# Reordering the start of a fused attention and MoE kernel by priorities, sharing one ring of buffers, and pairing its weighted sums

## The chip, the cores and the metric

The kernel runs on one core of one Trainium2 chip. The metric is the device time of one execution in microseconds (us); the kernel before took 1592.88 us, the median of three runs (1592.11 to 1593.0). The engines are TensorE (PE; its weight loads are shown as PEld), VectorE (DVE), ScalarE (ACT), GpSimd (POOL) and SyncE (SP). SP issues every transfer of this kernel, in one queue.

## The reference

Two layers of attention with 32 inducing points, and then a feed-forward block, over x of 4 batches of 12480 tokens of 128 channels:

```python
def mab(q, kv):
    s = scale * (q @ kv.transpose(0, 2, 1))
    s = s - s.max(-1, keepdims=True)
    a = np.exp(s)
    a /= a.sum(-1, keepdims=True) + 1e-09
    return a @ kv
h = mab(I, x)          # I: 32 x 128, the same for each batch; h: 32 x 128 a batch
y = mab(x, h)          # 12480 x 128 a batch
hid = y @ w_in         # 128 -> 2048
g = hid * (1.0 / (1.0 + np.exp(-1.702 * hid)))
out = g @ w_out        # 2048 -> 128
```

Everything is float32 on the device; w_in and w_out arrive as 64-bit floats and are decoded from their bits there. The first softmax runs over all tokens of a batch, so nothing of a batch's second softmax can start before h of that batch is known.

## The kernel before, in words

**Units.** A batch is cut into seven sups: six of 2048 tokens (four groups of 512, on four quarters of the partitions) and one of 192 (two groups of 96). A block is 512 tokens on their way through the feed-forward part. A batch gives 24 blocks, and the small sups of two batches make one more of 384 tokens, 98 blocks in all. y is never formed: y @ w_in is a @ (h @ w_in), so each batch needs `hw` = h @ w_in and the weights a of the second softmax, both as 32-bit values split into two fp32r parts and stacked on 128 partitions (`st` for a block, `hw` for a quarter of w_in).

**A block.** It has eight groups; a group `first(i)` (line 1022) makes two 128 x 512 hidden products into `ph`, ACT applies the gelu to get `g`, ACT or DVE rounds it to `hi`, and DVE takes the rest `lo`. `second(i, c)` (line 1052) adds three products to the block's output bank: hi with the low part of w_out, lo with the high part, hi with the high part. The first block (`WHOLE` = 8 groups) uses `g` and w_out undivided, as float32 products. `under_way` holds the half groups whose second products are still to be listed; `LAG` - 2 = 12 is the most, and the ring `ph_` has `LAG // 2` buffers each for hi and lo.

**Attention of a batch.** `attention(b)` (line 486) loads x transposed into the ring `px` (four buffers of one sup), makes the first scores `pa` with products of 32 output rows (four side by side, each on its own quarter of PE's columns), takes the maximum over all tokens (`max_turned`, `max_row`, `max_back`, `max_scaled`, lines 372 to 394), exponentials (`first_exponential`), transposes within 32 x 32 squares (`aT_of`), and a weighted sum `weigh` (line 409) against x by rows, which is loaded into the ring `pn` (two buffers), one sup after the other. `normalised` gives hT. `all_h_w_in` (line 592) makes `hw` of batches 1 to 3 and copies it into its stacked place by 16 transfers. `second_softmax` (line 562) makes second products in pairs of sups, and its exponentials four and three at a time.

**The start.** `start` (line 688) does the same for batch 0 with everything shown to it at once: x transposed stays in four buffers of `px` and two of its own, x by rows is made on the chip by PE's transposes for sups 0, 1, 2, 3 and 5 (`turning`, line 809; ACT copies them out), and loaded for sup 4 and the small one. The softmax is taken in two parts, sups 0 to 3 (`ES` = 4) with a first maximum and the others with the maximum over all; `joining` (line 867) rescales. The weights are decoded (`decode`, line 747) as their halves arrive, on ACT and DVE.

**What sets the order.** All instructions of an engine run in the order in which the program lists them. `Meter` and `Clocks` keep a planned time for each engine, from costs written in the kernel (`tensor_cost`, line 190). In the start, each piece of work is a generator that yields the engine and the tiles it needs next (`Jobs.add`). `Jobs.step` (line 145) lists the piece with the smallest planned time plus rank times 300 ns, over all engines. While PE would be idle by plan, `spin` (line 969) fills in dummy products `spun`, each charged 214 ns. After the start the main loop lists first and second groups and advances one generator, `attentions` (line 1090), a step a group; `until`, `room`, `deep` and `hop` hold it back. `deep` waits for a full queue of half groups before exponentials. `lay_out` (line 1119) runs the rest of it without pauses (`late`) if the weights of a sup are not there 14 groups ahead of their use.

Of the kernel before, what the change touches and what calls it, by code (L numbers as in the profile page):

```python
# [17 lines left out]
P = 128  # L18
# [4 lines left out]
LAG = 14  # L23
# [5 lines left out]
ES = 4  # L29
XB = 4  # L30
FB = 5
RANK = 300.0
# [98 lines left out]
class Jobs:  # L131
# [13 lines left out]
    def step(self, limit=None, but=None):  # L145
        best = None
        for job in self.threads:
            eng, tiles, when = job[1]
            if eng is but or when is not None and not when():
                continue  # L150
            t = max(eng.t, self.clocks.ready(*(tiles() if callable(tiles) else tiles)))
            if limit is not None and t > limit(eng):
                continue
            if best is None or t + job[2] * RANK < best[0]:
                best = t + job[2] * RANK, t, job
        if best is None:
            return False
        if self.idle:
            self.idle(best[1])
        job = best[2]  # L160
# [11 lines left out]
def set_attention_then_moe(ctx: ExitStack, tc, xT, x, indT, w_in, w_out, outT):  # L172
# [17 lines left out]
    def tensor_cost(name, out, w, x, **k):  # L190
        n = width(out)
        before, tiled[0] = tiled[0], out.shape[0] <= 32
        turn = 90 if before != tiled[0] else 0
        if x.dtype == F32R:
            return turn + max(107, 0.4548 * n)
        if name == "transpose":
            return turn + 0.85 * n
# [27 lines left out]
    NS = len(sups)  # L225
    EB = NS + 2
    on_chip = [s for s in range(NS - 1) if s != XB]

# [7 lines left out]
    pn = ctx.enter_context(tc.tile_pool(name="pn", bufs=2))  # L236
# [17 lines left out]
    rep2 = rep.rearrange("p g m -> p (g m)")  # L254
    one = const.tile([1, 1], F32, name="one")
# [17 lines left out]
    def deep():  # L273

        while len(under_way) < LAG - 2 and not late[0]:
            yield
# [32 lines left out]
    def load_xT(b, s):  # L309
        t0, g, w = sups[s]  # L310
        if g == G:
# [24 lines left out]
    def new_batch(b):  # L336
        a = SimpleNamespace(b=b, s1={}, aTs={})
# [29 lines left out]
    def first_max(a, s, scores):  # L367
        t0, g, w = sups[s]
        q = 32 * g
        dve.tensor_reduce(a.mx[0:q, s:s + 1], scores[0:q, 0:w], axis=AX.X, op=ALU.max)  # L370

    def max_turned(mx1):
        pa = ps_a.tile([P, 512], F32, tag="pa", name="pa")
        pe_.matmul(pa[0:1, 0:P], mx1, ident, start=True, stop=True)
        return pa

    def max_row(pa):
        row = psm.tile([1, M], F32, tag="row", name="row", bufs=1)
        dve.tensor_reduce(
            row, pa[0:1, 0:P].rearrange("p (g m) -> p m g", g=G), axis=AX.X, op=ALU.max  # L380
        )
        return row

    def max_back(row):
        pa = ps_a.tile([P, 512], F32, tag="pa", name="pa")
        for j in range(G):
            pe_.matmul(pa[32 * j:32 * j + 32, 0:1], row, one, start=True, stop=True)
        return pa

    def max_scaled(pa):  # L390
        nmx = psm.tile([P, 1], F32, tag="nmx", name="nmx")
        dve.tensor_scalar(nmx, pa[:, 0:1], -scale, None, op0=ALU.mult)
        return nmx

    def first_exponential(a, s, nmx):
# [3 lines left out]
        act.activation(e, e, AF.Exp, bias=nmx[0:q], scale=scale, accum_out=a.rs[0:q, s:s + 1])  # L399
# [86 lines left out]
    def attention(b):  # L486
# [26 lines left out]
        pa = max_turned(mx1)  # L513
        yield
        row = max_row(pa)
        yield from hop()
        pa = max_back(row)
# [8 lines left out]
        yield from until(dve, clocks.ready(a.s1[0][0]))  # L526
        yield from hop()
        pa = ps_a.tile([P, 512], F32, tag="pa", name="pa")
        aT_of(a, 0)
        xn = load_x(b, 0)  # L530
        yield from hop()
        i = 0
        for s in range(NS):
            if s == 2:
# [4 lines left out]
            if s + 1 < NS:  # L539
                yield from until(dve, clocks.ready(a.s1[s + 1][0]))  # L540
                yield from room()
                aT_of(a, s + 1)
                later = load_x(b, s + 1)
            yield from until(pe_, clocks.ready(a.aTs[s], xn))
            i = weigh(a, pa[:, 0:P], s, xn, i, blocks(range(NS)))
            xn = later
            yield from hop(3)
            if s < XB:
                again(b, s)
            yield from hop(3)  # L550
# [11 lines left out]
    def second_softmax(b, some):  # L562

        mine = {}
        for pair in pairs(some):
# [6 lines left out]
            pas = [second_products(b, s) for s in pair]  # L572
            yield
            for s, pa in zip(pair, pas):
                if s + XB < NS:
# [16 lines left out]
    def all_h_w_in(b):  # L592
# [6 lines left out]
        yield  # L599
# [9 lines left out]
        for c in range(G):  # L609
            t = phw.tile([P, 512], F32R, tag="hw", name="hw")  # L610
            for r in range(G):
                src = th.bitcast(F32) if r < G // 2 else tl
                sp.dma_start(
                    t[32 * r:32 * r + 32].bitcast(F32), src[32 * c:32 * c + 32]
                )
            hw[b, c] = t
            yield

# [69 lines left out]
    def start(pf, pw):  # L688
        a = new_batch(0)
        raws = []  # L690

        def load_out():

            t = pn.tile([P, BLK, P], F32, tag="xn", name="raw")
            for i in range(2):
                c = len(raws) - DFF // WC
                raws.append(t.rearrange("p k c -> p (k c)").bitcast(I32)[:, 2 * WC * i:2 * WC * (i + 1)])
                sp.dma_start(raws[-1], w_out[:, c * WC:(c + 1) * WC].bitcast(I32))

        for s in range(NS - 1):  # L700
            if s < DFF // WC:
                raws.append(pw.tile([P, 2 * WC], I32, tag="raw", name="raw", bufs=3))
                sp.dma_start(raws[s], w_in[:, s * WC:(s + 1) * WC].bitcast(I32))
            if s < XB:
                load_xT(0, s)
# [3 lines left out]
            if s == XB - 1:  # L709
                load_xT(0, NS - 1)  # L710
        turned = {}
        x5 = pn.tile([P, BLK, P], F32, tag="xn", name="xn")
        load_out()
        for s in range(XB, NS):
# [503 lines left out]
```

## Time and profile before

| | us |
|---|---|
| median of three runs | 1592.88 |
| span of the profiled execution, first to last instruction | 1591.5 |
| PE busy in it (matmuls are pipelined, so this is not PE at its peak) | 1580.0 |
| ACT busy | 1362.8 |
| DVE busy | 1318.4 |
| second products of batch 0 start at | 42.70 |
| first hidden product at | 50.51 |
| first divided product (hi with the low part of w_out) at | 72.66 |

The page gives no separate time for the profiled execution beside its span; the span lies 1.4 us below the median of the runs. In the rows below, "issue" names time in which an engine waited for nothing that the profile shows. Rows of groups have the count, the busy time, the mean of one in ns, and the idle time ahead with what ended it. All instructions listed through the `Meter` carry line 113, so tiles, not lines, tell them apart.

### The profile page before, as it was taken

To read this page: it belongs to the slowest core of one execution; us is meant where nothing else is said; L and a number is where in the kernel's file an instruction comes from. 1 tells how busy PE (TensorE), PEld (TensorE's weight loads), DVE (VectorE), ACT (ScalarE), POOL (GpSimd) and SP (SyncE) were. 2 spreads that over 40 slices of the span, in tenths; PEclk is the share of its full clock that TensorE was granted. 3 is DMA by queue.
4 is the path that set the end of the run, shared out by engine and by line. 5 is a ranking of instruction groups with operands and counts; after the bars stand their busy time and mean duration, and the time that the engine had idled before them with its cause. 6 is when DMAs were issued, how large, how long until landed. Compare 5 with 4: busy or idle time off the path is not lost.

```text
span 1591.5 us, 21955 instructions
## 1 busy us (share of the span) xinstructions
PE 1580.0 (99%) x7842; PEld 1236.7 (78%) x7842; DVE 1318.4 (83%) x1515; ACT 1362.8 (86%) x1573; POOL 0.7 (0%) x6
## 2 busy tenths in 40 slices
PE   9999999999999999999999999999999999999999
PEld 7667777777687778777777777777778788888887
DVE  6887987888888887788887887888878888888886
ACT  6789989987888888988888988988888998888885
POOL 0000000000000000000000000000000000000000
PEclk9999999999999999999999999999999999999999
DMA  7121415822242014731314112671311011111100
GB/s 270 60 65 69 155 34 114 189 58 55 83 162 78 21 47 109 172 87 35 105 44 175 49 34 51 149 165 37 93 44 48 24 42 41 35 32 40 39 29 20
DMA packets 85242, 125.71 MB, mean 79 GB/s; under 512 B 12176, under 2 KB 52880, under 8 KB 79504
## 3 DMA queue, kind: packets, MB, share of 16 engines
q1 hardware_dynamic: 85136, 124.32, 27.9%
q8 instruction: 64, 1.05, 0.3%
q14 instruction: 42, 0.34, 0.1%
HBM read 71.06 MB, written 25.56 MB: 61 GB/s over the span
## 4 chain that ended last, share of the span: by engine, by line
PE 96%; ACT 2%; DVE 1%; DMA 0%; issue 0%; SPq 0%; POOLq 0%; ACTq 0%; POOL 0%
PE pso L113 67%; PE ph L113 23%; PE pa L113 5%; PE spun L972 1%; ACT L113 1%; DVE lo L113 1%; DMA raw<-in_w_out 0%; ACT g L113 0%; PE h L113 0%; ACT hi L113 0%; ACT e L113 0%; DVE hi L113 0%; DVE e L113 0%; SPq L128 0%; DVE m L113 0%
## 5 line engine op out<-in xcount | busy, mean ns | idle before, releaser
L113 DVE TENSOR_TENSOR lo<-g,hi 128x1024 fp32r<-128x1024 f32 x776 | 939.0, 1217 | 162.8 <-ACT hi L113 148.1
L113 ACT ACTIVATE g<-ph 128x1024 f32<-128x1024 f32 (+1 forms) x784 | 810.4, 1038 | 180.0 <-PE ph L113 103.2
L113 PE MATMUL pso<-hi,wl 128*128 128x512 f32 (+1 forms) x1552 | 614.2, 396 | 0.0
L113 PE MATMUL pso<-lo,wh 128*128 128x512 f32 (+1 forms) x1552 | 608.1, 392 | 2.0 <-DVE lo L113 1.9
L113 PE MATMUL pso<-hi,wh 128*128 128x512 f32 (+1 forms) x1552 | 609.8, 393 | 0.0
L113 ACT ACTIVATE hi<-ph 128x1024 fp32r<-128x1024 f32 (+1 forms) x492 | 508.1, 1033 | 0.0
L113 PE MATMUL ph<-st,hw 128*128 128x512 f32 x1536 | 481.8, 398 | 2.7 <-ACT g L113 2.4
L113 PEld LDWEIGHTS pso<-hi,wl 128*128 128x128 f32 x1552 | 291.6, 188 | 82.3 <-issue 12.1
L113 PEld LDWEIGHTS ph<-st,hw 128*128 128x128 f32 x1536 | 286.5, 188 | 83.2 <-ACT g L113 12.4
L113 PEld LDWEIGHTS pso<-lo,wh 128*128 128x128 f32 x1552 | 291.8, 188 | 67.0 <-DVE lo L113 3.7
L113 PEld LDWEIGHTS pso<-hi,wh 128*128 128x128 f32 x1552 | 291.5, 188 | 66.7
L113 DVE CAST hi<-g 128x1024 fp32r<-128x1024 f32 x284 | 195.1, 687 | 75.9 <-ACT g L113 74.3
L113 ACT COPY ob<-pso 128x512 f32<-128x512 f32 (+1 forms) x98 | 59.2, 605 | 15.7 <-PE pso L113 15.7
L113 ACT ACT_TABLE_LOAD x30 | 38.5, 1283 | 1.2 <-PEq L1208 0.7
L972 PEld LDWEIGHTS spun<-ident 128*128 128x128 f32 x152 | 21.0, 214 | 7.0 <-issue 5.6
L113 PE MATMUL pa<-xt,hT 128*32 128x512 f32 x192 | 24.2, 600 | 1.7 <-DVE e L113 1.6
L972 PE MATMUL spun<-ident 128*128 128x128 f32 x152 | 23.5, 305 | 1.4 <-POOL ident masks.py:199 1.4
L113 PE MATMUL pa<-xt,indT_sb 128*32 128x512 f32 x192 | 23.7, 600 | 0.0
L113 PEld LDWEIGHTS pa<-xn,aT 128*32 128x32 f32 (+1 forms) x594 | 15.1, 109 | 7.7 <-issue 5.9
L113 PE MATMUL pa<-xn,aT 128*32 128x128 f32 (+1 forms) x594 | 20.7, 276 | 0.0
L113 DVE TENSOR_REDUCE mx<-s 128x1 f32<-128x512 f32 (+1 forms) x27 | 16.7, 621 | 4.0 <-ACT s L113 3.2
L113 ACT ACTIVATE e<-e 128x512 f32<-128x512 f32 (+1 forms) x28 | 14.5, 573 | 6.2 <-DVE e L113 6.1
(96 smaller groups left out, 400.6 us busy)
## 6 DMA issues: line engine op xcount, KB each, us to landing
xt<-in_xT SPq DMA_DIRECT2D x44, 1024.0 KB, 7.1
out_T<-ob SPq DMA_DIRECT2D x96, 256.0 KB, 2.0
xn<-in_x SPq DMA_DIRECT2D x72, 256.0 KB, 5.4
st<-ahT SPq DMA_DIRECT2D x184, 64.0 KB, 2.0
st<-alT SPq DMA_DIRECT2D x184, 64.0 KB, 2.0
raw<-in_w_in SPq DMA_DIRECT2D x4, 512.0 KB, 8.7
raw<-in_w_out SPq DMA_DIRECT2D x4, 512.0 KB, 11.5
hw<-th SPq DMA_DIRECT2D x24, 64.0 KB, 2.0
```

The costliest lines, as they stand in the source:

```text
L113: return f(*a, **k)
L972: nc.tensor.matmul(spun[:, 0:P], ident, ident, start=True, stop=True)
```

## The change

- **Priorities within an engine.** `Jobs.step` finds the piece that could start soonest, and among the pieces of that engine which could start within 300 ns after it takes the one with the lowest rank. Each piece has its own rank, from a table. The first block is listed by the same means (`undivided`, `undivided_seconds`), and fillers stop with its first hidden product.
- **Costs.** A change between full and 32-row products is charged 150 ns in place of 90, a transpose 0.93 ns a column in place of 0.85, a filler 265 ns in place of 214.
- **Loads and parts.** Another order of loads; w_out comes later than all of x, into buffers of transposed x that have been used; the small sup belongs to the first part of the softmax, sups 4 and 5 to the second. Sup 4 goes from PSUM straight into its exponential, and one half of a turn is copied by DVE. Weighing is a piece for each sup.
- **Maximum.** One product brings all partitions' maxima to every partition; DVE then takes the maximum of four, multiplies by a mask and adds up.
- **h @ w_in of batch 0** goes the way of the other batches, with 16 transfers.
- **One ring.** `pn` is gone; x by rows shares `px` with transposed x. `LAG` goes from 14 to 18; `deep` waits for 13 half groups.
- **Weighted sums of batches 1 to 3** are listed by (0, 1), (2, 3), (4, 5, 6). h @ w_in is listed right after the second products of one sup, exponentials five and two at a time, and laying out starts six groups later where the exponentials aren't listed.

The core of the diff:

```diff
-LAG = 14
+LAG = 18
+DEEP = 13
+LAST = -6
+SPIN = 265.0
+EARLY = (0, 1, 2, 3, 6)
+LATE = (4, 5)
+DIRECT = (4,)
+LOADS = "w0 3 w1 0 6 2 w2 1 4 5 w3 n4 n6"
+TURN_DVE = ((3, 8),)
+RANKS = {('maximum', 0): 5, ('maximum', 1): -2, 'joining': 2, 'first': -4, 'hw': -4, 'more': -1,
...
-            if best is None or t + job[2] * RANK < best[0]:
-                best = t + job[2] * RANK, t, job
...
+        soonest, job = min(able, key=lambda x: x[0])
+        eng = job[1][0]
+        t, job = min(
+            [x for x in able if x[1][1][0] is eng and x[0] <= soonest + WINDOW],
+            key=lambda x: (x[1][2], x[0]),
+        )
...
-        while len(under_way) < LAG - 2 and not late[0]:
+        while len(under_way) < DEEP and not late[0]:
...
-            t = pn.tile([P, BLK, P], F32, tag="xn", name="xn")
+            t = px.tile([P, SUP], F32, tag="xt", name="xn").rearrange("p (k c) -> p k c", c=P)
...
+    def max_everywhere(mx1):
         pa = ps_a.tile([P, 512], F32, tag="pa", name="pa")
-        pe_.matmul(pa[0:1, 0:P], mx1, ident, start=True, stop=True)
+        pe_.matmul(pa[:, 0:P], mx1.broadcast_to([P, P]), ident, start=True, stop=True)
         return pa
...
+        dve.tensor_mul(row, row, mine)
         nmx = psm.tile([P, 1], F32, tag="nmx", name="nmx")
-        dve.tensor_scalar(nmx, pa[:, 0:1], -scale, None, op0=ALU.mult)
+        dve.tensor_reduce(nmx, row, axis=AX.X, op=ALU.add)
...
+        for s in range(XB):
+            yield from until(pe_, clocks.free("xt", XB))
+            xns[s] = load_x(b, s)
+            yield
+        for some in ((0, 1), (2, 3), tuple(range(4, NS))):
...
+            for s in some:
+                yield from until(dve, clocks.ready(a.s1[s][0]))
                 yield from room()
+                aT_of(a, s)
+                yield from hop(2)
+            yield from until(pe_, clocks.ready(*[t for s in some for t in (a.aTs[s], xns[s])]))
+            for s in some:
+                i = weigh(a, pa[:, 0:P], s, xns[s], i, blocks(range(NS)))
...
+        def reloads():
+            for s, load in ((1, load_out), (2, load_out), (3, lambda: load_xT(0, 1))):
+                yield sp, [], has(("scores", s), *[("turned", s, k) for k in (0, 8) if s in on_chip])
+                load()
+                done.add(("reload", s))
...
+        def first_h_w_in():
+
+            yield pe_, lambda: [hTs[0], *w_in_sb], bank("pa", "h", *[("w_in", c) for c in range(DFF // WC)])
+            pa = h_w_in_parts(0)
+            hold("pa")
+            yield act, [pa], None
+            th = pt.tile([P, 512], F32R, tag="t", name="th")
+            act.copy(th, pa)
+            yield dve, [th], None
+            tl = pt.tile([P, 512], F32, tag="t", name="tl")
+            dve.tensor_sub(tl, pa, th.bitcast(F32))
+            hold("pa", -1)
+            for c in range(DFF // WC):
+                yield sp, [tl], None
+                copies_of_hw(0, c, th, tl)
+                done.add(("hw", c))
...
+    def undivided(i):
+
+        yield pe_, lambda: [stacks[0, 0, 0], hw[0, i // 2]], bank(
+            "ph", ("stack", 0), ("hw", i // 2), ("first", i - 1), ("second", i - AHEAD)
+        )
+        ph = hidden(i)
...
+    def undivided_seconds():
+
+        while under_way:
+            i, c = under_way[0]
+            what = ("w_out", (2 * i + c) // 4)
+            yield pe_, lambda: [parts[i][0], whole[(2 * i + c) // 4]], has(("g", i), what)
+            second(*under_way.pop(0))
+            done.add(("second", i))
...
-            yield from all_h_w_in(b)
-            yield from second_softmax(b, turn[0:4])
+            yield from second_softmax(b, turn[0:5], True)
             yield from hop(6)
-            yield from second_softmax(b, turn[4:])
+            yield from second_softmax(b, turn[5:])
...
-            if back is None and turns and i >= begin[turns[0]]:
+            if back is None and turns and i >= begin[turns[0]] - LAST * (turns[0] not in es):
```

More of the change, by code (lines that the diff above doesn't have):

```diff
@@ L192, in tensor_cost @@
         before, tiled[0] = tiled[0], out.shape[0] <= 32
-        turn = 90 if before != tiled[0] else 0
+        turn = 150 if before != tiled[0] else 0
         if x.dtype == F32R:
@@ L512, in attention @@
         yield from hop()
[L513 to L517, printed above, removed]
+        pa = max_everywhere(mx1)
         yield
@@ L525, in attention @@
         yield
-        yield from until(dve, clocks.ready(a.s1[0][0]))
-        yield from hop()
         pa = ps_a.tile([P, 512], F32, tag="pa", name="pa")
-        aT_of(a, 0)
-        xn = load_x(b, 0)
-        yield from hop()
         i = 0
-        for s in range(NS):
-            if s == 2:
+        xns = {}
+        for s in range(XB):
[3 more added lines that the diff above has]
+        for some in ((0, 1), (2, 3), tuple(range(4, NS))):
+            if some[0] == 2:
                 yield from deep()
@@ L538, in attention @@
                 yield
-            if s + 1 < NS:
-                yield from until(dve, clocks.ready(a.s1[s + 1][0]))
+            for s in some:
+                yield from until(dve, clocks.ready(a.s1[s][0]))
                 yield from room()
[L542 to L550, printed above, removed]
+                aT_of(a, s)
[3 more added lines that the diff above has]
+                i = weigh(a, pa[:, 0:P], s, xns[s], i, blocks(range(NS)))
+            yield from hop(2)
+            for s in some:
+                if s + XB < NS - 1:
+                    xns[s + XB] = load_x(b, s + XB)
+                elif s == 2:
+                    t = pt.tile([P, TOK // P, P], F32, tag="t", name="xn_last")
+                    xns[NS - 1] = load_x(b, NS - 1, t)
+                if s != NS - 1 and s > 1:
+                    again(b, s - 2)
+                yield from hop(2)
         hu = psm.tile([P, P], F32, tag="hu", name="hu", bufs=1)
@@ L560, in attention, with second_softmax @@
         yield from hop()
-    def second_softmax(b, some):
+    def second_softmax(b, some, with_hw=False):
         mine = {}
-        for pair in pairs(some):
+        some = list(some)
+        for pair in [some[0:1]] * with_hw + pairs(some[with_hw:]):
             while full(pair):
@@ L572, in second_softmax @@
             pas = [second_products(b, s) for s in pair]
+            if with_hw and pair[0] == some[0]:
+                parts_of_hw = h_w_in_parts(b)
+                yield
+                yield from all_h_w_in(b, parts_of_hw)
             yield
             for s, pa in zip(pair, pas):
-                if s + XB < NS:
+                if b == 0 and s == 1:
+                    for r in range(3, NS - 1):
+                        load_xT(0, r)
+                        yield
+                elif b and s + XB < NS:
                     again(b, s + XB)
@@ L1034, in first @@
                 )
-        if i < WHOLE:
-            g = ph_.tile([P, 2, TOK], F32, tag="hi", name="g")
-            act.activation(g, ph, AF.Gelu_apprx_sigmoid)
-            parts[i] = g, g
-            return
+        return ph
+    def first(i):
+        ph = hidden(i)
+        n = sum(p[2] for p in work[i // NG][1])
         hi = ph_.tile([P, 2, TOK], F32R, tag="hi", name="hi")
@@ L1088, in set_attention_then_moe @@
     po = ctx.enter_context(tc.tile_pool(name="po", bufs=2))
+    done.update([("first", -1)] + [("second", -i) for i in range(1, AHEAD + 1)])
+    under_way += [(i, c) for i in range(WHOLE) for c in range(2)]
+    stores = []
+    for i in range(WHOLE):
+        jobs.add(undivided(i), rank("undivided"))
+    jobs.add(undivided_seconds(), rank("seconds"))
+    while ("first", 0) not in done:
+        jobs.step()
+    jobs.idle = None
+    while ("g", WHOLE - 1) not in done:
+        jobs.step()
+    jobs.threads[:] = [t for t in jobs.threads if t[0].gi_code is not undivided_seconds.__code__]
     def attentions():
```

272 lines of the change are left out of this document (132 added, 140 removed).

## The prediction, made before the changed kernel was built or run

> **What bounds the kernel now.** I read the page's busy shares and chain first, then PE's own waits, then five stretches of the span.
>
> ```profile
> span 1591.5 us, 21955 instructions
> PE 1580.0 (99%) x7842; PEld 1236.7 (78%) x7842; DVE 1318.4 (83%) x1515; ACT 1362.8 (86%) x1573; POOL 0.7 (0%) x6
> ...
> PE 96%; ACT 2%; DVE 1%; DMA 0%; issue 0%; SPq 0%; POOLq 0%; ACTq 0%; POOL 0%
> ```
>
> PE is in the chain for 96% of the span. That isn't yet a full PE: matmuls are pipelined, and idle-looking fillers count as busy. What PE waits for by name is little:
>
> ```profile
> PE ph L113 <- ACT g L113: 2.4, 2, 1.2
> PE pso L113 <- DVE lo L113: 1.9, 3, 0.8
> PE pa L113 <- DVE e L113: 1.6, 1, 1.6
> ```
>
> So a gain must come from fewer or cheaper PE instructions, or from the start, where PE spins on dummy products. By stretches (columns: us, then busy us and count of PE, PEld, DVE, ACT, POOL, then PE clock, DMA share, GB/s): before h is known, from h to the first hidden product, block 0, and a stall.
>
> ```profile
> 0.00:42.30 42.30, 40.94 (x481) 33.45 (x482) 26.62 (x68) 25.26 (x44) 0.70 (x6) 1.00 0.75 255
> 42.30:50.50 8.20, 7.92 (x47) 5.02 (x46) 7.56 (x17) 4.47 (x8) 0.00 (x0) 1.00 0.69 241
> 50.50:72.66 22.16, 20.96 (x70) 11.58 (x69) 18.59 (x33) 19.40 (x29) 0.00 (x0) 1.00 0.02 7
> ...
> 91.00:99.20 8.20, 6.21 (x19) 4.16 (x17) 5.87 (x9) 8.16 (x10) 0.00 (x0) 0.79 0.08 32
> ```
>
> In the first 42.3 us DVE is busy 26.6 and ACT 25.3: neither is the bound; order is. The chain of that time (start us, us, what):
>
> ```profile
> 1.36 9.41 PE spun L972 x60
> ...
> 30.90 0.31 PE pa L113 x2
> ...
> 32.23 0.17 PE pa L113 x8
> 32.40 1.01 PE h L113 x32
> ...
> 34.05 2.76 PE h L113 x96
> 36.81 1.09 PE spun L972 x8
> 37.90 2.23 PE h L113 x70
> 40.13 1.09 PE spun L972 x8
> 41.22 0.39 PE pa L113 x4
> ...
> 42.70 1.10 PE pa L113 x8
> ...
> 53.20 0.74 PE ph L113 x2
> ...
> 61.86 2.58 PE pso L113 x6
> ```
>
> A spin is two records. The old list charges it 214 ns; here four take 1.09 us (272 ns), thirty at the start 9.41 (314 ns). The list puts PE ahead of where it is.
>
> **The change, part by part.**
>
> *Until h (second products start at 42.70).* Loads first:
>
> ```profile
> 0.00:10.00 10.00, 8.64 (x55) 8.65 (x56) 5.02 (x18) 2.79 (x4) 0.70 (x6) 1.00 0.78 280
> 10.00:20.00 10.00, 10.00 (x84) 7.12 (x84) 7.13 (x13) 7.31 (x11) 0.00 (x0) 1.00 1.02 414
> ```
>
> ```profile
> 22.00:24.00 2.00, 2.00 (x21) 1.12 (x19) 1.83 (x5) 1.66 (x4) 0.00 (x0) 1.00 1.00 418
> ...
> 28.00:30.00 2.00, 2.00 (x16) 1.04 (x17) 0.72 (x3) 0.81 (x2) 0.00 (x0) 1.00 1.23 194
> ...
> 32.00:34.00 2.00, 2.00 (x50) 1.50 (x47) 1.50 (x5) 1.55 (x6) 0.00 (x0) 1.00 0.31 60
> ```
>
> By 20 us 2.80 + 4.14 = 6.94 MB are in. By their shapes x transposed (6.39 MB) and w_in (2.10 MB) are 8.49 MB: at 415 GB/s they end near 23.7. Half of w_out (1.05 MB) follows, then x by rows for sups 4 and 6 (1.15 MB) at some 180 GB/s until about 33. The change takes w_out out of that line, so the rows start at 23.7 and end near 30. Earliest end of the first phase, then: rows of sup 6 at 30.0, the last weighings (37.90, 2.23 us) 32.2, and from there to second products as now (40.13 to 42.70, 2.57) 34.8: at most 7.9 us sooner. ACT is tighter: of its 25.26 us 2.79 were done by 10 us; a copy goes (sup 4 is exponentiated from PSUM) and a turn goes to DVE, about 1.6 together, so 20.9 remain. At the 88% that ACT reaches in block 0 (19.40 of 22.16) they take 23.7, to 33.7; with a transpose (0.7), one weighing (1.0) and the same 2.57 second products start at 38.0, 4.7 sooner. The two-product maximum (0.31 + 0.17 on PE with a DVE reduction between) becomes one product and three DVE operations; one crossing less, about half a microsecond, inside this term. Spins charged 265 ns instead of 214 no longer push PE late. Low end: nothing, or a list that orders things worse, 2 us lost, the size of two spin groups now standing in this stretch (36.81 and 40.13). I take -4.5, the ACT bound with a little left over.
>
> The Trainium skill, in "DMA: Bandwidth & Descriptors", section "Where 436 GB/s comes from", puts a core's loads from HBM at about 358 GB/s. The trace differs with its 414 to 418. By 358 the 5.7 MB left at 10 us would end 2.2 us later, the earliest second products would be at 37.0, and this term nearer -3.5; the trace's rate decides.
>
> *From h to the first hidden product, 8.2 us.* h times w_in changes from four full products with copies to one bank of four column tiles, one ACT copy, one DVE subtraction and 16 copies by SP. On the page and in the timeline:
>
> ```profile
> hw<-th SPq DMA_DIRECT2D x24, 64.0 KB, 2.0
> ```
>
> ```profile
> 396.68 1.22 SPq L128 DMA_DIRECT2D hw<-th  x2
> ```
>
> Four issues at 0.61 and 2.0 us to land: 1.1 (second products) + 1.0 (product) + 0.6 (copy) + 0.7 (subtraction), with some 0.8 of latencies, + 3 x 0.61 + 2.0 gives 8.0 after 42.7: as late as the stack, which sets 50.5 now. Chunk k is ready 2.4 us after chunk k-1, while two groups take longer than that. Queued ahead of these copies on SP is one megabyte load (2.5 us at 415 GB/s), issued some 3 us sooner. Bounds -0.5 to +1.5; I take 0. Three of the old products also leave PE, but fillers stood between them.
>
> *Block 0 (22.16 us).* Its floor on PE: sixteen undivided products at 0.86 (61.86: six records in 2.58), eight pairs of hidden products at 0.46, three stacks at 0.4 (four records, like 41.22), and the first wait for ACT (53.20) 1.6: 20.3. ACT had 19.40 us here, partly decoding w_out; the second half of w_out was loaded only after 44 us and now comes near 35 with the first. That work then fits into ACT's idle time before block 0 (4.47 of 8.20 busy). Bounds -1.9 and +2 (decodes that land in DVE's busy 7.56 of 8.20 instead); I take -1.5.
>
> *The stall at 91 to 99.*
>
> ```profile
> 91.60 0.40 PE L113 MATMUL pso<-hi,wh 128*128 128x512 f32 x1
> 93.21 0.72 PE L113 MATMUL ph<-st,hw 128*128 128x512 f32 x2 [1.22 <-ACT g L113]
> ...
> 98.97 0.39 PE L113 MATMUL pso<-hi,wl 128*128 128x512 f32 x1
> ```
>
> ```profile
> 650.78 5.55 PE pso L113 x24
> ```
>
> ```profile
> 96.00:98.00 2.00, 2.00 (x6) 1.54 (x6) 1.97 (x3) 1.97 (x3) 0.00 (x0) 0.50 0.34 131
> ```
>
> Thirteen products start from 91.60 up to 98.97; at 0.231 (24 in 5.55) they need 3.0, they took 7.4: 4.4 us lost, part of it because the granted clock fell to 0.50 after PE had waited. It is one exponential with two table loads on ACT while the queue of hidden groups was short. The queue now holds 16 half groups instead of 12, exponentials wait for 13, and PE enters block 1 with a better stocked queue. Bounds -4.4 and +1; I take -3.3, for the exponential itself still falls near here.
>
> *Fewer tiled visits, batches 1 to 3.* One visit of 32-column products:
>
> ```profile
> 80.70 0.63 PE L113 MATMUL ph<-st,hw 128*128 128x512 f32 x2
> 81.25 1.06 PE L113 MATMUL pa<-xt,hT 128*32 128x512 f32 x8
> ...
> 83.04 0.63 PE L113 MATMUL ph<-st,hw 128*128 128x512 f32 x2
> 83.50 0.39 PE L113 MATMUL pso<-hi,wl 128*128 128x512 f32 x1
> ```
>
> A pair of hidden products takes 0.46 when a plain product follows and 0.55 when a tiled one does: 0.09 to enter. Weighing 32 products takes 1.01, 96 take 2.76, so 0.875 for each further 32 and 0.135 fixed. A visit costs 0.225. Weighing goes from seven visits a batch to three (12 fewer in all, 2.7 us); h times w_in joins the first second-products (3 fewer, 0.7); of the two maximum visits (0.31 and 0.17, each with its entry) one full product like that at 41.22 (0.39 for four records, so some 0.2 to 0.26) remains: 0.4 a batch, 1.2. Sum -4.6; between -2.8 (if the entry is only the reading of the records) and -5.2. Cover: DVE's two extra small operations and the held-back transposes lie beside PE, with DVE 83% busy; uncovered they are some 0.4 us a batch. The one ring makes x wait on SP for buffers of transposed x, with the output's stores queued behind; it is asked for after the first products, which free them, so I cost it at nothing, and at one late load (5 us, once) if that is wrong.
>
> *Other waits.* Of PE's named waits 1.6 (pa for DVE) and about 1.1 lie after 99 us. The deeper queue, bursts of five and two exponentials for four and three, and the later forced laying out may take them away or move them. Bounds -2.7 to +4; I take -1.5.
>
> Sum: -4.5 + 0 - 1.5 - 3.3 - 4.6 - 1.5 = -15.4. The profiled execution's span is 1591.5, 1.4 below the median of the runs, 1592.9; that margin stays, so 1577.5.
>
> **The rivals.**
>
> A. *The first phase doesn't give* (the listing doesn't do what it says): rows of sup 6 and h stay chained to the same loads, since SP issues the rows only as its queue drains. For: the rows move at some 180 GB/s and the last weighing waits for them. Against: nothing was being moved after 34 and the last weighing began at 37.90. Then only visits, and half of the stalls, are left: -4.6 - 2.5 = -7, so 1586.
>
> B. *Slower: batch 1 is laid out in a lump.* Laying out now starts six groups later where the exponentials aren't ready. Should weighing end later than now, one sweep does five sups' second softmax without pauses. From the groups:
>
> ```profile
> L113 DVE STREAM_TRANSPOSE e<-pa 128x512 f32<-128x512 f32 x24 | 17.0, 710 | 0.2 <-PE pa L113 0.2
> ```
>
> Five sups times three DVE operations of about 0.7 are 10.5 us, 5 exponentials and two table loads some 5, normalising and copies 8: 24 us against 8 groups of 1.85 (15 us) left, so PE starves 9 us, and cools for about 2 more. Two batches have that deadline (block 24 and its like): 22 us, with -15 from the rest: 1600. For: 1.6 us of it stand in the trace now (pa for DVE). Against: it decides only if weighing slips by more than the room it has now, and it has fewer pauses than before.
>
> C. *The clock falls in the start.* Fillers get fewer and stop at the first hidden product. The row 96 to 98 shows that a PE with gaps loses half its clock; products then take twice their time for a few microseconds. Two such falls in block 0 cost 2 x 2 and eat that term: 1583. Against: with 20.96 of 22.16 busy, the clock read 1.00.
>
> The Trainium skill, "TensorE: Matmul & The Clock Gate", section "What's actually happening", has this rule: a PE idle over a window of some 3.4 us is halved until a busy window follows. The fall at 94 agrees with it in kind, after 1.6 us of standstill and thin work around.
>
> **How the numbers follow.** Forecast (-10 to -22, so 1571 to 1583): 0.56. A: 0.16. C: 0.08. B: 0.10. No change within 0.2% (3.2 us, what a measurement can tell here): 0.10, where small losses in the lists, or that late load, eat the visits. All better ends together are -22.7, so 1570; the range goes from 1569 to 1590 and leaves out B and some of no change. Faster: 0.56 + 0.16 + 0.08 = 0.80; same 0.09; slower 0.10 and 0.01 of the last case, 0.11.
>
> **What would show it.** Second products at 36 to 40 instead of 42.70; the first undivided hidden product 8 us later; the first divided product (72.66 now) near 66.5; no product at half clock near 90; three weighing visits a batch, the first of 64 products in 1.9 us; PE's named waits after 100 us under 2 us. Wrong if second products start after 41, if block 0 takes over 23 us, or if PE stands still for more than 2 us near 400 or 1150.

## The result, and the profile after

| | before | after |
|---|---|---|
| median, us | 1592.94 (1592.11 to 1593.44) | **1581.42** (1580.67 to 1583.44) |
| executions | 4 | 4 |

The ratio is 0.9931, with a 95% interval from 0.9918 to 0.9945: 11.5 us faster, where 15.4 were forecast. The profiled execution of after is the slowest of its four; the others have spans of 1578.9, 1579.5 and 1579.8. The page of after:

```profile
span 1581.7 us, 21787 instructions
...
PE 1567.6 (99%) x7764; PEld 1235.7 (78%) x7764; DVE 1322.4 (84%) x1527; ACT 1357.2 (86%) x1560; POOL 0.7 (0%) x6
...
PE 95%; DMA 1%; DVE 1%; SPq 1%; ACT 1%; issue 0%; ACTq 0%; DVEq 0%
```

PE has 12.4 us less busy time in 78 fewer instructions, and is still the chain. What PE waits for by name in after (us in total, times, longest):

```profile
PE ph L127 <- DMA st<-alT: 2.7, 1, 2.7
PE pa L127 <- DVE two L127: 2.2, 2, 1.5
PE pso L127 <- DVE whole L127: 1.8, 2, 1.1
...
PE h L127 <- DMA xf_last<-in_x: 1.1, 1, 1.1
PE pso L127 <- DVE lo L127: 0.6, 1, 0.6
```

Of these before had 0.2 of the wait for `two` and 1.9 of that for `lo`, nothing of the others. All of them lie ahead of 230 us, and behind that point no named wait of PE is left in after. Over the stretches of after (same columns as in the prediction: until the second products, to the first hidden product, block 0 in three parts, the place of the old stall, and a new one):

```profile
0.00:38.00 38.00, 35.29 (x416) 28.13 (x416) 27.60 (x70) 24.10 (x42) 0.70 (x6) 1.00 0.99 332
38.00:45.30 7.30, 6.55 (x56) 4.95 (x56) 6.73 (x16) 3.92 (x6) 0.00 (x0) 1.00 0.67 226
45.30:52.10 6.80, 5.66 (x22) 3.32 (x21) 5.92 (x15) 5.48 (x9) 0.00 (x0) 1.00 0.35 85
52.10:62.50 10.40, 8.19 (x20) 4.36 (x19) 7.50 (x14) 5.65 (x9) 0.00 (x0) 0.67 0.04 11
62.50:73.00 10.50, 10.50 (x31) 5.66 (x30) 4.39 (x5) 9.60 (x13) 0.00 (x0) 1.00 0.00 0
91.00:99.00 8.00, 8.00 (x37) 6.47 (x36) 6.67 (x7) 7.59 (x8) 0.00 (x0) 1.00 0.09 33
160.00:190.00 30.00, 26.46 (x113) 19.16 (x113) 22.29 (x29) 26.02 (x31) 0.00 (x0) 0.94 0.57 195
```

The first phase gained, the stall at 91 is gone (37 records in 8.0 us, where 19 took 8.2), block 0 lost, and between 160 and 190 there is a stall that before didn't have. To place gains and losses I use ACT's copy of a block's output, `ob<-pso`. For blocks 0 and 9 these rows are, in before:

```profile
74.87 0.59 ACT L113 COPY ob<-pso 128x512 f32<-128x512 f32 x1
...
226.77 0.60 ACT L113 COPY ob<-pso 128x512 f32<-128x512 f32 x1
```

and in after:

```profile
72.76 0.59 ACT L127 COPY ob<-pso 128x512 f32<-128x512 f32 x1
...
226.77 0.63 ACT L127 COPY ob<-pso 128x512 f32<-128x512 f32 x1
```

2.1 us are gained by the end of block 0, none is left at the end of block 9, and the stretch from there to the end falls from 1364.7 to 1354.9: so all of the profiled difference, 9.8 us, comes after block 9. The same marks from each run's profiled execution (start of second products, first hidden product, first divided product; then block 0's output to block 9's, and from there to the end of the span):

| run | second products | first hidden | first divided | blocks 0 to 9 | 9 to end |
|---|---|---|---|---|---|
| before | 42.70 | 50.51 | 72.66 | 151.9 | 1364.7 |
| after | 38.04 | 45.33 | 73.02 | 154.0 | 1354.9 |
| e2_nodecode | 38.05 | 45.33 | 68.24 | 150.1 | 1354.8 |
| e3_out1 | 41.70 | 50.37 | 71.19 | 149.9 | 1355.4 |
| e9_more | 40.07 | 47.35 | 69.93 | 152.6 | 1354.9 |
| e7_half | 40.39 | 48.78 | 71.15 | 153.8 | 1354.9 |
| e1_last0 | 37.81 | 46.32 | 70.62 | 151.6 | 1355.3 |
| e10_first | 37.71 | 46.43 | 71.73 | 150.5 | 1355.3 |
| e5_queue | 38.19 | 45.50 | 71.86 | 149.2 | 1356.2 |
| e4_single | 37.76 | 45.05 | 69.78 | 154.1 | 1361.3 |
| e6_spin | 38.46 | 47.22 | 71.50 | 152.3 | 1354.9 |
| a0_after | 38.49 | 46.89 | 72.86 | 153.9 | 1354.8 |
| c1_queue_more | 38.03 | 46.48 | 71.67 | 147.9 | 1356.1 |
| c2_queue_out1 | 40.93 | 49.62 | 70.45 | 148.1 | 1356.1 |

### The profile page after: what moved, and what is told of

The parts are those of the page before. It is cut to its first block, busy times and chain, and to the rows that moved or that the text cites. A ratio compares the mean times of both kernels' runs of the same rounds, so it can differ in the third digit from the quotient of the medians.

```text
span 1581.7 us, 21787 instructions
## 1 busy us (share of the span) xinstructions
PE 1567.6 (99%) x7764; PEld 1235.7 (78%) x7764; DVE 1322.4 (84%) x1527; ACT 1357.2 (86%) x1560; POOL 0.7 (0%) x6
## 4 chain that ended last, share of the span: by engine, by line
PE 95%; DMA 1%; DVE 1%; SPq 1%; ACT 1%; issue 0%; ACTq 0%; DVEq 0%
PE pso L127 68%; PE ph L127 23%; PE pa L127 4%; SPq L142 1%; DMA xt<-in_xT 1%; DMA xf_last<-in_x 0%; DMA st<-alT 0%; DVE lo L127 0%; DVE sm L127 0%; ACT L127 0%; ACT e L127 0%; DVE e L127 0%; PE h L127 0%; ACT g L127 0%; DVE tmp L127 0%
## 5 line engine op out<-in xcount | busy, mean ns | idle before, releaser
L127 ACT ACTIVATE hi<-ph 128x1024 fp32r<-128x1024 f32 (+1 forms) x486 | 501.6, 1032 | 0.0
L127 PEld LDWEIGHTS ph<-st,hw 128*128 128x128 f32 x1536 | 287.4, 188 | 82.3 <-issue 11.5
L127 DVE CAST hi<-g 128x1024 fp32r<-128x1024 f32 (+1 forms) x290 | 199.2, 687 | 75.2 <-ACT g L127 74.1
L127 PE MATMUL pso<-g,whole 128*128 128x512 f32 x32 | 18.5, 686 | 1.8 <-DVE whole L127 1.8
L1001 PEld LDWEIGHTS spun<-ident 128*128 128x128 f32 x114 | 16.3, 226 | 4.1 <-issue 2.7
L1001 PE MATMUL spun<-ident 128*128 128x128 f32 x114 | 17.7, 316 | 1.4 <-POOL ident masks.py:199 1.4
L127 DVE TENSOR_TENSOR e<-e,sm 128x512 f32<-128x512 f32 (+3 forms) x29 | 17.8, 613 | 1.0
L127 DVE TENSOR_REDUCE m<-e 128x16 f32<-128x512 f32 (+1 forms) x28 | 17.4, 623 | 1.0
L127 DVE STREAM_TRANSPOSE e<-pa 128x512 f32<-128x512 f32 (+1 forms) x28 | 18.1, 646 | 0.1
```

The source lines that it names most:

```text
L127: return f(*a, **k)
L1001: nc.tensor.matmul(spun[:, 0:P], ident, ident, start=True, stop=True)
```

## The experiments

Behind each measured time stand the lowest and the highest execution, and the ratio to the kernel before on the same chip with its 95% interval. Runs on different chips are compared by these ratios. Readings of stages come from one profiled execution of each run.

### Block 0: is it the decoding of w_out?

PE and DVE in block 0 of after:

```profile
47.65 1.10 PE L127 MATMUL pso<-g,whole 128*128 128x512 f32 x2 [1.15 <-DVE whole L127]
...
54.63 0.63 PE L127 MATMUL pa<-ident_r,two 128*128 128x128 f32 x4 [1.53 <-DVE two L127]
55.94 2.08 PE L127 MATMUL pso<-g,whole 128*128 128x512 f32 x2 [0.67 <-DVE whole L127]
58.66 3.55 PE L127 MATMUL pso<-g,whole 128*128 128x512 f32 x4
62.51 1.88 PE L127 MATMUL pso<-g,whole 128*128 128x512 f32 x4
```

```profile
46.82 0.68 DVE L127 SCALAR_TENSOR_TENSOR whole<-tmp 128x512 f32<-128x512 f32 x1
...
54.59 1.29 DVE L127 SCALAR_TENSOR_TENSOR whole<-tmp 128x512 f32<-128x512 f32 x2
...
58.70 0.69 DVE L127 SCALAR_TENSOR_TENSOR whole<-tmp 128x512 f32<-128x512 f32 x1
```

ACT takes the first two raw quarters of w_out as they land, during the last weighing, when h is nearly done:

```profile
34.16 0.71 ACT L127 ACTIVATE tmp<-raw 128x512 f32<-128x512 f32 x1 [0.37 <-DMA raw<-in_w_out]
35.44 0.67 ACT L127 ACTIVATE tmp<-raw 128x512 f32<-128x512 f32 x1 [0.57 <-DMA raw<-in_w_out]
```

Each quarter (`whole`) is ready only inside block 0, DVE does the decoding between the pieces of the second softmax (`two`), and PE stands behind both in the order of its own list. After the waits, the four records from 58.66 take 3.55 us, where the same four from 62.51 take 1.88: half clock. e2 leaves the decoding of w_out out:

```diff
+            if name[0] == "w_out":
+                yield dve, [raw], None
+                dve.tensor_scalar(out.bitcast(I32), h, 0xFFFFF, 0x3C000000, op0=ALU.bitwise_and, op1=ALU.bitwise_or)
+                done.add(name)
+                return
```

> The changed kernel with the decoding of w_out left out: one DVE operation a quarter stands for six on DVE and two on ACT, so the values of w_out are wrong. Theory 1 (block 0 is long because the decoding of all four quarters now falls into it, on DVE, and PE stands behind two and whole): from the first hidden product to the first divided product 20 to 22 us instead of 27.7, no product at half clock, 6 to 7 us less in all, about 1575. Rival (PE is held by the order of its own list in block 0, the stacks and the undivided products): 26 us or more, less than 2 us gained.

Measured, one execution: 1573.05. Block 0 of e2:

```profile
45.30:68.20 22.90, 22.59 (x81) 12.13 (x79) 8.74 (x13) 19.01 (x27) 0.00 (x0) 1.00 0.14 35
```

PE stands for 0.3 us, at full clock, and handles ten records more than after did in 27.7: eight tiled products (1.06) and a further hidden pair (0.46). Without these it is 21.4, so the decoding costs block 0 some 6.3 us, about half of it the clock: e4 below, with the same two waits of 2.2 and 1.8 and a clock of 1.00 throughout, took 24.7. The stall at 178 went too. Whether that is because block 0 ends 6.3 us sooner stays open, for PE's later products also come in another order in e2; in e3, e4, e6, e7 and e9 below, block 0's output comes 0.4 to 3.2 us sooner than in after, and the wait for `st` stays (2.4 to 2.8 us).

Can the decoding be done earlier? Or can PE's list be put in a better order beside it? e3 lists the second quarter of w_out ahead of other work, e9 lists the other three stacks of sup 0 behind the undivided products, and e7 puts x by rows behind the first half of w_out, as before had it.

```diff
-RANKS[('out', 1)] = 7
+RANKS[('out', 1)] = 0
```

> The changed kernel with one rank changed: the second quarter of w_out is decoded ahead of the third (rank 0 for 7). Theory 1 (decoding on DVE sets block 0): the wait for whole at 55.9 and for two at 54.6 (0.7 and 1.5 us) mostly go, products keep full clock, block 0 3 to 5 us shorter; but the earlier decoding can delay h by up to 3 us on DVE. Together 1578 to 1582. Rival (PE's own list sets block 0): block 0 stays at 27 us and the kernel gets slower by what h loses.

Measured: 1579.67 (1576.58 to 1582.14), 0.9917 [0.9902, 0.9932]. Block 0 takes 20.8 (with one hidden pair fewer), but second products come 3.7 us later: the decoding is moved into the first phase, where it delays h.

```diff
-RANKS['more'] = -1
+RANKS['more'] = 7
```

> The changed kernel with one rank changed: the stacks of block 0's other three groups after the undivided products (rank 7 for -1). Theory 1 (PE stands behind two at 52 to 55 since the stacks are listed ahead of products that could run, and the clock falls from it): the wait of 1.5 us for two goes and no product runs at half clock; block 0 24 to 25 us instead of 27.7; 1577 to 1580. Rival (decoding sets it, PE would wait for whole instead): waits for whole grow to 2 us or more, block 0 stays over 26, within 1 us of 1581.4.

Measured: 1579.16 (1578.8 to 1581.0), 0.9919 [0.9905, 0.9934]. Block 0 takes 22.6, with the transposes of one stack fewer (0.4); second products come 2.0 later. That isn't the change's doing: PE, DVE and ACT have the same instructions in the same order ahead of them as in after. In this execution PE stood 2.0 us for the rows of sup 6 (they landed at 33.58, in after at 33.12), and then the clock was low during the last weighing (0.72 over the 6 us from 32). The same 64 products, in after and then in e9:

```profile
33.60 1.95 PE L127 MATMUL h<-xf,aT 128*32 128x128 f32 x64
```

```profile
34.29 3.29 PE L127 MATMUL h<-xf,aT 128*32 128x128 f32 x64
```

c1 below has the same rank, and its second products start at 38.03.

```diff
-LOADS = "w0 3 w1 0 6 2 w2 1 4 5 w3 n4 n6"
+LOADS = "w0 3 w1 0 6 2 w2 1 4 5 w3"
+BY_ROWS = (4, 6)
...
                 load()
+                if s == 1:
+                    for r in BY_ROWS:
+                        ...
+                        turned[r] = load_x(0, r, t)
```

> The changed kernel with the first half of w_out loaded ahead of x by rows, after sup 1 is used. Theory 1 (decoding in block 0 costs what it costs because w_out comes behind the rows): the rows and so second products come 1.5 to 3 us later (about 40 instead of 38.0), and block 0 gets 2 to 5 us shorter (22 to 25 from the first hidden to the first divided product, 27.7 now); 1579 to 1582. Rival (the list, not the arrival, puts the decoding there): second products later by the same, block 0 unchanged, 1583 to 1585.

Measured: 1583.42 (1579.93 to 1586.15), 0.9943 [0.9924, 0.9961]. Block 0 takes 22.4, second products start 2.4 later and the first hidden product 3.5 later. All three shorten block 0. e3 and e7 pay for it in the first phase, where the decoding of a quarter of w_out, or the load of half of it, delays h; e9 changes only the order behind h and doesn't pay there. So both have a part: PE waits for the decoding, and the order of its list sets how much of that it feels. By their intervals none of the three is told from after in the whole time.

### The stalls at 91 and 178: which part did what?

```diff
-LAST = -6
+LAST = 0
```

> The changed kernel with forced laying out at the old point (LAST 0 for -6), all else the same. Theory 1 (starting to lay out six groups later pushes the weights of batch 0's third sup onto SP behind three loads, so PE waits for stacked weights at 178 to 182 and then runs at half clock): the wait of PE for st there, 2.7 us, goes, with the slow products after it and the 0.6 and 0.3 us before it, so 3 to 5 us faster than the changed kernel, about 1577.5; the waits of the old kernel near 400 (1.6) may come back. Rival (the loads ahead of the stacked copies on SP are what is late, not the point of laying out): the wait stays at 2 us or more and the time stays within 1 us of 1581.4.

Measured: 1579.44 (1578.69 to 1581.24), 0.9918 [0.9904, 0.9933]. PE's rows of e1 near 91:

```profile
90.80 0.73 PE L127 MATMUL ph<-st,hw 128*128 128x512 f32 x2 [1.22 <-ACT g L127]
...
92.78 0.50 PE L127 MATMUL pso<-lo,wh 128*128 128x512 f32 x1 [0.76 <-DVE lo L127]
```

The old stall is back with the queue of 18 in place, and the wait for `st` at 178 is gone: the laying out six groups later removed the one and, with the queue of 18 (e5 below), made the other. From block 0's output to block 1's takes 17.6 in after and 22.1 in e1, but PE handles nine more records there in e1 (89 for 80); at the prediction's 0.231 they are 2.1, so the stall itself costs e1 some 2.4, at a clock of 1.00. In before the clock fell as well. The rival fell, too: in e1 the first stacked copy also goes behind three loads and takes 9.3 us to land (161.39 to 170.72), but it is issued 11.5 us sooner than in after (2.4 of it from block 0), and PE doesn't wait. By the medians e1 is 2.0 below after, not 3 to 5, with the old stall back; the intervals overlap.

e10 keeps the six groups for the first laying out alone, batch 0's own other sups excepted:

```diff
-begin[turns[0]] - LAST * (turns[0] not in es)
+begin[turns[0]] - LAST * (turns[0] == (0, 1) and turns[0] not in es)
```

> The changed kernel with laying out six groups later only for batch 0's second sup; for all others at the old point. Theory 1 (the later point removes the stall near 91, where an exponential meets a short queue, and makes the one near 178, where the weights come too late): neither stall is there, 1576.5 to 1578.5, 3 to 5 us faster than the changed kernel and 1 to 3 faster than the old point everywhere (1579.4). Rival (the two stalls come of where attention stands against the blocks, and move with any change): a stall of 2 us or more stands in another place before 200 us, no faster than 1579.

Measured: 1579.24 (1578.82 to 1580.48), 0.9919 [0.9904, 0.9934]. Neither stall is there, and blocks 0 to 9 take 150.5 instead of 154.0. But e1, which differs only in that one laying out, takes 151.6 for the same 683 records of PE, and the two ratios are alike (0.9918 and 0.9919). So against the old point the removal of the stall at 91 brings about 1.1 in the profile and nothing that the medians show, less than the 1 to 3 of theory 1; in e10 PE stands 0.16 and 0.77 us near 155 instead, a small form of what the rival said, whose time it has.

e5 takes the old queue back:

```diff
-LAG = 18
-DEEP = 13
+LAG = 14
+DEEP = 12
```

> The changed kernel with the old queue (LAG 14 for 18, deep at 12 for 13). Theory 1 (laying out, not the queue, removes the stall near 91; a deeper queue only covers bursts of exponentials): no stall near 91, but the bursts of five show waits of PE for lo or g of 0.5 to 1 us each, four or five of them; 1582 to 1586. Rival (the deeper queue is what removed that stall): it comes back with 4 us, and PE waits for g there as in the old kernel; 1586 or more. Rival (the queue does nothing): within 1 us of 1581.4.

Measured: 1578.85 (1578.13 to 1579.2), 0.9914 [0.9898, 0.9931]. The deeper queue was expected to help, and it doesn't. With the old queue, the window of the old stall and that of the new one are full in e5:

```profile
90.00:99.00 9.00, 9.00 (x41) 7.29 (x40) 6.64 (x6) 8.56 (x10) 0.00 (x0) 1.00 0.08 29
...
160.00:190.00 30.00, 29.45 (x141) 20.83 (x141) 25.98 (x31) 27.94 (x32) 0.00 (x0) 1.00 0.56 193
```

The five exponentials in row form for the other sups, in e5 and then in after:

```profile
156.81 2.37 ACT L127 ACTIVATE e<-e 128x512 f32<-128x512 f32 x5
```

```profile
161.70 2.37 ACT L127 ACTIVATE e<-e 128x512 f32<-128x512 f32 x5
```

They come 4.9 us later with the queue of 18, where they wait for 13 half groups; 1.16 of it is block 0's (in e1, without the six groups, they come at 150.18). What follows in after, on SP and PE:

```profile
169.18 3.55 SPq L142 DMA_DIRECT2D xt<-in_xT  x3
172.91 0.51 SPq L142 DMA_DIRECT2D st<-ahT  x1
```

```profile
181.63 2.05 PE L127 MATMUL ph<-st,hw 128*128 128x512 f32 x4 [2.68 <-DMA st<-alT]
```

Three loads of 1 MB are issued in a row, then the stacked weights: the first such copy takes 7.9 us to land (as a rule 2.0). In e5 one load goes at 167.01 and the next at 177.35, between the copies. Outputs of blocks 0 to 5 come at the same spacing in both runs (e5 1.16 us ahead throughout); at block 9 e5 is 5.99 ahead. So the stall costs 4.8 us: the wait of 2.7, and a clock of 0.94 over the 30 us. After block 9 the old queue loses 1.3. The effect on the median is 2.6, and the two intervals overlap. But the wait for `st` stands in each run with both the queue of 18 and the later laying out, except e2 (after, a0, e3, e4, e6, e7, e9: 2.4 to 2.8 us), and in none where either is taken back (e1, e5, e10, c1, c2). In blocks 0 to 9, c1 below is 4.7 shorter than e9; c2 is only 1.8 shorter than e3, where the wait of 2.8 brought no fall of the clock (1.00 from 160 to 190).

### The visits

e4 makes the weighted sum of batches 1 to 3 one sup at a time again, seven visits for three:

```diff
-        for some in ((0, 1), (2, 3), tuple(range(4, NS))):
+        for some in tuple((r,) for r in range(NS)):
```

> The changed kernel with the weighted sums of batches 1 to 3 one sup a visit again (seven visits a batch for three, loads in the same ring). Theory (a visit costs PE 0.225 us): twelve visits more, 2.7 us slower than the changed kernel, 1584, with no new waits of PE. Rival (the entry of 0.09 us is only a reading of the records, 0.135 a visit): 1.6 us slower. Rival (pairing pays by something else, such as fewer pauses and less waiting for laying out): 4 us or more slower, with waits of PE by name near the starts of batches.

Measured: 1586.65 (1585.54 to 1589.45), 0.9964 [0.995, 0.9978]; 5.2 more than after. The stretch after block 9 goes from 1354.9 to 1361.3, 6.4 more. PE's waits of e4 after 230 us and the longer place of them:

```profile
PE pa L127 <- DVE e L127: 2.2, 2, 1.2
```

```profile
405.89 2.26 PE L127 MATMUL pa<-xt,hT 128*32 128x512 f32 x16 [1.16 <-DVE e L127]
409.16 1.06 PE L127 MATMUL pa<-xt,hT 128*32 128x512 f32 x8 [1.01 <-DVE e L127]
```

2.2 of the 6.4 is a wait like the one that stood in before near 399; 2.7 is what twelve visits were to cost. PE handles the same 6545 records after block 9 in both and is busy 4.1 longer in e4 (1355.2 for 1351.1): 0.34 a visit, where 0.225 was forecast. Why a visit costs more than its rows showed stays open. So four visits fewer in a batch save PE's own time, and a wait besides. A first visit of after has 64 products in 1.96 us:

```profile
272.30 1.96 PE L127 MATMUL pa<-xn,aT 128*32 128x128 f32 x64
```

### The first phase: fillers or loads?

The chain of after until h (start, us, what):

```profile
26.50 6.62 DMA xf_last<-in_x
33.26 2.30 PE h L127 x70
...
38.04 1.11 PE pa L127 x8
```

The last weighing waits for x by rows of sup 6, which lands at 33.1. e6 charges the fillers as before:

```diff
-SPIN = 265.0
+SPIN = 214.0
```

> The changed kernel with a filler charged 214 ns again. Theory 1 (fillers charged too little push PE late in the first phase): second products at 38.5 to 40 instead of 38.0, 0.5 to 2 us slower. Rival (PE is no longer late by fillers, since the chain until h now runs through the last load and DVE): second products within 0.3 of 38.0, the time within 1 us of the changed kernel's beside it.

Measured: 1581.43 (1580.36 to 1584.27), 0.9938 [0.9925, 0.9952]; second products at 38.46, and 38.49 with the charge of 265 on the same chip. The charge does nothing that these runs can tell.

### After again, and two combinations

> The changed kernel itself again, beside the three below on one chip. Theory 1 (the profiled run shown first had a fall of the clock in block 0 that the typical run has not, worth some 2 us): a time of 1580 to 1582 and, in most runs, a span near 1579 at a clock of 0.999; the wait for st near 178 is there in any case. Rival (the fall belongs to every run): spans near 1581.7 at 0.997.

Measured, on the chip of e6: 1581.81 (1578.48 to 1583.15), 0.9929 [0.9916, 0.9941]. Neither expectation is met cleanly: executions with a mean clock of 0.998 have spans of 1580.0 to 1581.3, one at 0.999 has 1578.4, and the one at 1.000 has 1576.7. Both profiled executions of this kernel have the fall, in block 0 and again behind the wait at 178 (in a0 1.7 us are lost at each place). Where it lies in the others is not recorded; those at 0.998 are 3.3 to 4.6 us longer than the one at 1.000.

c1 joins e5 and e9, c2 joins e5 and e3.

> The old queue (LAG 14, deep at 12) and the stacks of block 0 after the undivided products, together. Theory 1 (a deeper queue brings the hidden products, and so the stacked weights, two groups earlier, which makes the wait near 178; the stacks' place sets the waits of block 0; the two are apart): both gains add, 2.3 and 2 us, 1576 to 1578, with no wait for st. Rival (the wait for st depends on where block 0 ends): block 0 ends sooner and the wait is back with 2 us or more, 1578.5 or more.

Measured: **1575.99** (1575.53 to 1579.34), 0.9901 [0.9887, 0.9914]. Its waits in the profile:

```profile
PE ph L127 <- ACT st L127: 1.5, 1, 1.5
...
PE pa L127 <- DMA xt<-in_xT: 1.0, 1, 1.0
...
PE ph L127 <- DMA hw<-tl: 0.9, 1, 0.9
PE pa L127 <- DVE two L127: 0.7, 1, 0.7
```

The wait for `st` copied by DMA and those for `whole` are gone, and blocks 0 to 9 take 147.9. The profiled execution, at 1579.34, still has the fall of the clock in block 0 (0.87 over it); the other three, at a mean clock of 1.000, have spans of 1573.8 to 1574.3 against its 1577.5.

> The old queue (LAG 14, deep at 12) and the second quarter of w_out decoded ahead of the third. Theory 1 (as for the stacks: two gains that add): h 3 to 4 us later, block 0 near 21 us, no wait for st near 178, 1576 to 1578.5. Rival: the wait for st is back, 1579 or more.

Measured: 1577.59 (1576.53 to 1579.31), 0.9907 [0.9894, 0.9921], with second products at 40.93. Both combinations are below after on the same chip by their medians, 5.8 and 4.2; c1 is the fastest complete kernel of this study. c1's interval lies wholly below that of after on the same chip (0.9916 to 0.9941), c2's overlaps with it.

## Why the prediction was right or wrong

Direction and range held, but that is in part luck. Block 0 lost 5.5 us where a gain of 1.5 was forecast, and a stall that the sum didn't have cost 4.8; the sum was no more than 3.9 us too good because the stretch after block 9 gave 3.7 more than its terms. (The better ends of the terms add up to -22.6, not -22.7, which changes nothing.)

**Until h (-4.5).** Measured -4.66, second products at 38.04 for 38.2. The size was right by luck and the reason wrong: the sum let the rows of sup 6 be in at 30.0 and took ACT as the bound. They landed at 33.1, and the last weighing, 4.8 us ahead of the second products, started then. It is 4.6 sooner than in before (37.90); with the rows behind half of w_out (e7) it started at 35.60, so w_out's place is worth about half of that. The other half is not the load's: in before the rows had landed at 34.91, 3.0 us ahead of the last weighing. Which part of the new order brings it, no run separates. The charge for fillers, named inside this term, is worth nothing (e6). By the 358 GB/s of the Trainium skill ("DMA: Bandwidth & Descriptors", "Where 436 GB/s comes from") the term was estimated at -3.5; it was more, but as the rows decided and not the bulk of x, this doesn't test that figure.

**h to the first hidden product (0).** 7.81 before, 7.29 after; a0 has 8.40. As the working had it, the copies of `hw` land at the edge: eight of the thirteen profiled executions with the change (c1's row above is one) wait 0.7 to 1.2 us for them; there they, and not the stack, set the start.

**Block 0 (-1.5).** This step failed: 22.15 before, 27.69 after, 24.7 where the clock held (e4). The prediction's own sign of being wrong, over 23 us, came true. Two mistakes. The floor counted eight pairs of hidden products, but twelve stand before the first divided product (24 records, as in before): 20.3 + 4 x 0.46 = 22.1, which is what before took, so there was little to gain from cover: some 0.8, by e2's 21.4 and e3's 20.8 + 0.46. And the decoding of w_out was to fit into ACT's idle time ahead of block 0. The first raw quarter comes in at 34.1 (ACT's row above), but DVE, not ACT, carries most of the decoding, and DVE was already full there (6.73 of 7.30). The upper bound of this term, +2, named just that and was too small: it left out that PE's list holds PE behind `two` and `whole`, and the clock. Rival C has its mechanism here, in part: the clock did fall in block 0, for 3.0 us in the profiled execution of after (27.7 less e4's 24.7) and less in a0; but it ate a gain that was hardly there.

**The stall at 91 (-3.3).** Gone: 37 records in the 8 us. By the prediction's reading it was worth 4.4 in before, with the clock's fall; in e1, at a clock of 1.00, it costs some 2.4, and e10, without it, is 1.1 ahead of e1 at block 9. But the step put the gain down to the queue, and e1 and e5 show that the queue has no part in it: the exponential is simply laid out six groups later (in after it runs at 99.19, in before at 90.19).

**Fewer visits (-4.6) and other waits (-1.5).** Together -6.1; the stretch after block 9 holds nearly all of it and fell by 9.8. e4's 6.4 less its wait of 2.2 are 4.2 for twelve visits that were priced at 2.7: the price was too low, and the wait that pairs avoid wasn't in it. The named waits of before after 230 us, 2.7, are all gone. Of the remaining 2.5 of the 9.8 (9.8 - 4.6 - 2.7), 1.5 are the visits at e4's price; 1.0 has no row of its own. From 235 us, where both kernels stand at the same block, the windows are, of before:

```profile
235.00:1591.00 1356.00, 1350.23 (x6530) 1067.03 (x6528) 1128.90 (x1244) 1168.96 (x1330) 0.00 (x0) 1.00 0.28 74
```

and of after:

```profile
235.00:1581.00 1346.00, 1342.91 (x6509) 1070.18 (x6507) 1132.87 (x1256) 1163.57 (x1320) 0.00 (x0) 1.00 0.28 74
```

PE's busy time falls by 7.3 and its standing (5.8 to 3.1) by 2.7: so the part beyond the forecast is in the busy time, with the visits.

**What the sum didn't have.** A stall of 4.8 at 178, a mild form of rival B's mechanism at another place: work laid out later meets a deadline. There it was batch 1's exponentials on DVE and ACT; here it is the copies of batch 0's stacked weights behind three loads. The prediction put the ring's loads at nothing, because x is asked for after the products that free its buffers, and at one late load of 5 us "if that is wrong". It was the right place (the ring's loads on SP) and, by chance, the right price, with another victim: the copies queued behind the loads, not the loads.

By stretches: forecast -6.0 to the end of block 0 and -3.3 for the stall; measured -2.1 (-5.3 in e4, where the clock held) and, with the new stall inside, +2.1; then -9.8 for -6.1. Rival A fell with second products at 38.04, though what it named is there: the last weighing waits 1.1 us for the rows of sup 6. "No change" fell too.

## What to carry to other kernels

Before crediting a stage with cover, count every instruction listed before its milestone, and ask of work moved out of a load's way which engine does it in the next stage and whether an in-order neighbour then waits behind it; if it does, listing other ready work ahead of the wait (e9) left the first phase alone, where moving the work forward (e3, e7) delayed it. A rule like "wait until the queue is full" with a deeper queue delays whatever waits for it: look at what that work must be ahead of. And before issuing several large loads in a row, look for small urgent copies that the same queue will get next.

## What the hardware showed unexpectedly

- Gaps of 0.7 to 1.5 us on PE around 47 to 56, with thin work between, went with a granted clock of 0.67 over the 10.4 us from 52.1 in one execution of after, and of 1.00 in e4, whose waits are the same. The gaps seem needed (e2, without them, keeps 1.00) and are not enough; what decides stayed open. The Trainium skill ("TensorE: Matmul & The Clock Gate", "What's actually happening") speaks of an idle window of some 3.4 us; no single gap ahead of this fall is longer than 1.53, nor ahead of the one at 94 in before (1.22 and 0.77), which the prediction called an agreement in kind. Executions of the same kernel spread over 4.7 us (1578.48 to 1583.15 in a0), the slower ones at the lower mean clock.
- A 64 KB copy issued right after three 1 MB loads on one queue took 7.9 us to land instead of 2.0 (9.3 in e1).
- In the first phase x by rows moves slowly although the DMA engines read as full:

```profile
26.00:28.00 2.00, 2.00 (x67) 1.79 (x58) 1.72 (x5) 1.98 (x6) 0.00 (x0) 1.00 1.23 191
...
30.00:32.00 2.00, 2.00 (x43) 1.74 (x34) 1.65 (x7) 1.47 (x5) 0.00 (x0) 1.00 1.05 245
```

191 to 245 GB/s at a DMA share over 1, while mostly rows were moved, against 414 for x transposed in the prediction's row at 10 to 20. The last of the rows is in the chain from its issue at 26.50 to its landing at 33.1.
